# Attention with a gated MLP on one core: a planned order of the engines' queues, and part of the softmax exponentials computed on VectorE

## The chip, the cores and the metric

One core of a Trainium2 chip runs the whole program. The metric is the device time of one execution in microseconds (us). TensorE (PE) multiplies, ScalarE (ACT) computes functions such as the exponential, VectorE (DVE) does element-wise work, GpSimd (POOL) a little of it, SyncE (SP) issues most transfers.

## The reference

```python
def _A_ref(x, wqkv, wo):                      # S = 2048, D = 640, H = 32, Dh = 20
    qkv = (x @ wqkv).reshape(B, S, 3, H, Dh)  # -> q, k, v
    p = softmax(einsum("bhqd,bhkd->bhqk", q, k) * Dh ** -0.5)
    return einsum("bhqk,bhkd->bhqd", p, v).reshape(B, S, D) @ wo
def _B_ref(x, w1, b1, w2):                    # F = 1536
    h = einsum("bsd,df->bsf", x, w1) + b1
    return einsum("bsf,fd->bsd", h * tanh(softplus(h)), w2)     # Mish
g = sigmoid((x * gate_w).sum(-1, keepdims=True))
return g * _A_ref(x, wqkv, wo) + (1 - g) * _B_ref(x, w1, b1, w2)
```

All tensors are bf16. The softmax needs 32 x 2048 x 2048 exponentials.

## The kernel before

Four heads are taken together (`p`, 8 packs), each in 32 partitions, and 512 query columns (`qc`, 4 chunks): 32 groups. In a group, 16 key tiles of 128 (`j`) times 4 heads (`t`) make 64 units; a unit is a 128x512 block of scores. Units are taken alternately three and two at a time. One such iteration is a score step on PE (L568; up to four heads sit in different rows of the array and run together) into one of two PSUM tiles, and one exponential on ACT (L578). The 4 heads of a key tile are then multiplied with V in one V step (L609; four column strips together), summed in the PSUM tile `acc`. V carries a column of ones, so the sum of the exponentials comes out too. After 16 key tiles the group is transposed on DVE, divided and transposed back (`normalise`, L584).

Everything else is "chains" on PE: Q and K (L243) and V (L264) projections, the first MLP product (L327), the second (L356) and the output projection (L393). Each chain fills one of two PSUM tiles (`pp`), which DVE empties. A chain has a start and a due time in iterations; `pump` (L541) issues, after each iteration, as many chain pieces as the shares ask for, at most 700 ns of them. The Mish of each 128x512 block of `h` is spread over the following iterations (L289): an exponential on ACT, then on DVE a polynomial, four reciprocals (L304) and products.

PE, ACT and DVE each work their queues in order, so an instruction that waits holds all behind it.

Of the kernel before, what the change touches and what calls it, by code (L numbers as in the profile page):

```python
# [9 lines left out]
P = 128  # L10
# [3 lines left out]
BF16 = mybir.dt.bfloat16  # L14
PSUM = bass.MemoryType.PSUM


class Chain:

    def __init__(self, start, due, pieces, finish, ready=None, hard=True):
        self.start, self.due, self.pieces, self.finish = start, due, deque(pieces), finish
        self.ready = ready or (lambda: True)
        self.hard = hard
        self.cost = sum(c for c, _ in pieces)

    def share(self, i):
        if i >= self.due:
            return self.cost  # L30
        if i <= self.start:
            return 0.0
        return self.cost * (i - self.start) / (self.due - self.start)
# [3 lines left out]
def kernel(  # L37
# [26 lines left out]
    WIDTHS = (3, 2)  # L64
    N_CAP = 1.0e30
# [19 lines left out]
    actp = ctx.enter_context(tc.tile_pool(name="actp", bufs=16))
    outp = ctx.enter_context(tc.tile_pool(name="outp", bufs=2))
# [23 lines left out]
    w1t = {}  # L110

    def load_strip(kind, p, eng):
        t = wsp.tile([P, KT, 4 * DH], BF16, tag=f"ws{kind}", name="ws")
        c0 = kind * D + p * 4 * DH
        eng.dma_start(out=t[:, :, :], in_=wrows[:, :, c0 : c0 + 4 * DH])  # L115
        strips[(kind, p)] = t

    def load_w1(k):
        if k < 4 * NQC:
            i = k % 4  # L120
            w1t[k] = w1p.tile([P, KT, 3 * P], BF16, tag="w1t", name="w1t")
# [12 lines left out]
    for c in range(1, NQC):  # L134
        nc.sync.dma_start(
            out=xs[c][:, :, :],
            in_=x2d[c * QC : (c + 1) * QC, :].rearrange("(u p) d -> p u d", p=P),
        )
# [16 lines left out]
    for t in (wqp[1], wkp[1], T2[0], T2[1]):  # L155
        nc.gpsimd.memset(t, 0.0)
# [10 lines left out]
    first = {}  # L167
    for G, (p, qc) in enumerate(groups):
        first.setdefault(p, G)
    units = [  # L170
        (G, p, qc, j, t)
        for G, (p, qc) in enumerate(groups)
        for j in range(NS)
        for t in range(4)
    ]
    iters = []
    pos = 0
    while pos < len(units):
        n = min(WIDTHS[len(iters) % len(WIDTHS)], len(units) - pos)
        iters.append((pos, n))  # L180
        pos += n
    NI = len(iters)
    it_of = [0] * len(units)
    for i, (a, n) in enumerate(iters):
        for k in range(a, a + n):
            it_of[k] = i

    def it_at(G, j=0):
        k = G * 64 + 4 * j
        return it_of[k] if k < len(units) else NI  # L190

    kT = {}
    qT = {}
    OT = {}
    Bt = {}
    act = {}
    later = []
    seq = [0]
    in_mish = [0]
    b_done = [0] * NQC  # L200
    normalised = set()
    x_ready = [NU] + [0] * (NQC - 1)

    def at(i, fn):
        seq[0] += 1
        later.append((i, seq[0], fn))

    now = [0]


    def mm_pieces(n, fn, each):
        return [(each, (lambda k=k: fn(k))) for k in range(n)]

    def transpose_tile(c, u, ps, eng):
        s = NU * c + u
        for kt in range(KT):
            nc.tensor.transpose(  # L217
                ps[:, kt * P : (kt + 1) * P], xs[c][:, u, kt * P : (kt + 1) * P], ident
            )
        dst = xT[:, :, s * P : (s + 1) * P]  # L220
        src = ps[:, 0 : KT * P].rearrange("p (k q) -> p k q", q=P)
        if eng is nc.scalar:
            nc.scalar.copy(out=dst, in_=src)
        else:
            eng.tensor_copy(out=dst, in_=src)  # L225

    def transpose_chain(c, u, start, due):
        def piece():
            ps = pp.tile([P, KT * P], BF16, tag="pp", name="ps")
            transpose_tile(c, u, ps, nc.vector)  # L230
            x_ready[c] += 1

        return Chain(start, due, [(400, piece)], lambda: None)

    def kq_chain(wpad, chunk, get_dst, start, due, before=None, copy=None):
        box = {}

        def piece(kt):
            if kt == 0:
                if before is not None:  # L240
                    before()
                box["ps"] = pp.tile([P, QC], F32, tag="pp", name="ps")
# [3 lines left out]
                rhs=xT[:, kt, chunk * QC : (chunk + 1) * QC],  # L246
# [4 lines left out]
        def finish():  # L251
            (copy or nc.vector.tensor_copy)(out=get_dst(), in_=box["ps"][:, :])  # L252

        return Chain(start, due, mm_pieces(KT, piece, 215), finish, lambda: x_ready[chunk] == NU)

    def v_chain(sts, w, c0, n, start, due, gate=False):
        box = {}
        width = n + (1 if gate else 0)

        def piece(k):  # L260
            i, kt = divmod(k, KT)
            if k == 0:
                box["ps"] = pp.tile([P, len(sts), width], F32, tag="pp", name="ps")
# [9 lines left out]
        def finish():  # L273
            h0 = 0 if gate else c0 // DH
            nh = n // DH
            for i, st in enumerate(sts):
                nc.vector.tensor_copy(
                    out=VA[:, st, h0 : h0 + nh, 0:DH],
                    in_=box["ps"][:, i, 0:n].rearrange("p (h d) -> p h d", d=DH),
                )  # L280
            if gate:
                nc.vector.tensor_copy(
                    out=z_t[:, sts[0] : sts[0] + len(sts)], in_=box["ps"][:, :, n]
                )

        return Chain(start, due, mm_pieces(KT * len(sts), piece, max(40, width / 2.3)), finish,
                     lambda: all(x_ready[st // NU] == NU for st in sts))

    def mish_steps(ft, c, h):  # L289
        e = mp.tile([P, QC], F32, tag="e", name="e")  # L290
        r = mp.tile([P, QC], F32, tag="r", name="r")
        nc.scalar.activation(e[:, :], h[:, :], ACT.Exp)  # L292

        def first_ops():
            nc.vector.scalar_tensor_tensor(  # L295
                out=e, in0=e, scalar=2.0, in1=e, op0=ALU.add, op1=ALU.mult
            )
            nc.vector.tensor_scalar(
                out=r, in0=e, scalar1=N_CAP, scalar2=2.0, op0=ALU.min, op1=ALU.add
            )  # L300

        def rec(k):
            a, b = k * P, (k + 1) * P
            nc.vector.reciprocal(out=r[:, a:b], in_=r[:, a:b])  # L304

        def last_ops():
            nc.vector.scalar_tensor_tensor(
                out=r, in0=e, scalar=N_CAP, in1=r, op0=ALU.min, op1=ALU.mult
            )
            t = actp.tile([P, QC], BF16, tag="act", name="act")  # L310
            nc.vector.tensor_tensor(out=t, in0=h, in1=r, op=ALU.mult)
            act[(ft, c)] = t
            in_mish[0] -= 1

        at(now[0] + 1, first_ops)
        for k in range(4):
            at(now[0] + 2 + k, (lambda k=k: rec(k)))
        at(now[0] + 6, last_ops)

    def h_chain(ft, c, start, due):  # L320
        box = {}

        def piece(kt):
            if kt == 0:
                in_mish[0] += 1
                box["ps"] = pp.tile([P, QC], F32, tag="pp", name="ps")
            nc.tensor.matmul(  # L327
                box["ps"][:, :],
                lhsT=w1t[4 * c + ft // 3][:, kt, (ft % 3) * P : (ft % 3 + 1) * P],
# [3 lines left out]
            )  # L333

        def finish():
# [5 lines left out]
            if ft % 3 == 2:  # L341
                load_w1(4 * c + ft // 3 + 2)
# [397 lines left out]
```

## Time and profile before

| | |
|---|---|
| time, median of 3 runs | 1138.24 us (1133.45 to 1138.47) |
| span of the profiled execution | 1130.1 us; its own time is not given apart from the span |
| mean granted TensorE clock | 0.667 of 2.4 GHz |
| busy: PE, ACT, DVE, POOL | 1036.3, 992.6, 490.7, 16.2 us |
| PE matmuls / ACT / DVE instructions | 5545 recorded / 873 / 767 |

An engine's busy time is the union of its instructions; PE's matmuls are pipelined, so steps are better read by the distance of their starts. The granted clock is 1.00 (2.4 GHz) or 0.50 (1.2 GHz) at any moment; a value between is a mean over a stretch.

### The profile page before, as it was taken

To read this page: it belongs to the slowest core of one execution; us is meant where nothing else is said; L and a number is where in the kernel's file an instruction comes from. 1 tells how busy PE (TensorE), PEld (TensorE's weight loads), DVE (VectorE), ACT (ScalarE), POOL (GpSimd) and SP (SyncE) were. 2 spreads that over 40 slices of the span, in tenths; PEclk is the share of its full clock that TensorE was granted. 3 is DMA by queue.
4 is the path that set the end of the run, shared out by engine and by line. 5 is a ranking of instruction groups with operands and counts; after the bars stand their busy time and mean duration, and the time that the engine had idled before them with its cause. 6 is when DMAs were issued, how large, how long until landed. Compare 5 with 4: busy or idle time off the path is not lost.

```text
span 1130.1 us, 13823 instructions
## 1 busy us (share of the span) xinstructions
PE 1036.3 (92%) x5545; PEld 267.9 (24%) x5616; DVE 490.7 (43%) x767; ACT 992.6 (88%) x873; POOL 16.2 (1%) x26
## 2 busy tenths in 40 slices
PE   6898789999899999989999999899999989998996
PEld 3322221123212112321111123111112321212232
DVE  3336675612665655225665532465556211011123
ACT  4988998889988888998888899988988998889896
POOL 2000000000000000000100000000000000000000
PEclk8866965579656555985555589555556975557688
DMA  8000001000010001000020000000000000000000
GB/s 252 2 1 18 18 1 26 18 1 1 1 25 18 18 1 25 1 1 18 1 54 18 11 15 1 1 18 17 1 1 1 1 1 12 7 12 6 13 19 30
DMA packets 31272, 19.35 MB, mean 17 GB/s; under 512 B 14056, under 2 KB 31208, under 8 KB 31208
## 3 DMA queue, kind: packets, MB, share of 16 engines
q1 hardware_dynamic: 28664, 17.60, 5.7%
q10 hardware_dynamic: 2544, 0.86, 0.3%
q8 instruction: 44, 0.72, 0.3%
q14 instruction: 20, 0.16, 0.1%
HBM read 15.84 MB, written 2.62 MB: 16 GB/s over the span
## 4 chain that ended last, share of the span: by engine, by line
PE 64%; ACT 22%; issue 11%; DVE 2%; DMA 1%; SPq 0%; ACTq 0%; DVEq 0%
PE Sp L568 24%; ACT E L578 21%; PE acc L609 15%; PE ps L243 8%; PE ps L327 7%; PE ps L393 4%; PE ps L264 3%; PE ps L356 2%; ACT e L292 1%; DMA b1bf<-in_B_b_dram 1%; DMA ws<-in_A_wqkv_dram 0%; DVE r L304 0%; SPq L115 0%; PE ps L217 0%; DVE ot L699 0%
## 5 line engine op out<-in xcount | busy, mean ns | idle before, releaser
L578 ACT ACTIVATE E<-Sp 128x1536 bf16<-128x1536 f32 (+1 forms) x819 | 967.9, 1245 | 113.3 <-PE Sp L568 67.0
L568 PE MATMUL Sp<-qT,kT 32*128 32x512 bf16 x2048 | 430.1, 519 | 71.1 <-ACT E L578 55.2
L609 PE MATMUL acc<-E,VA 128*21 128x512 bf16 x2048 | 270.9, 519 | 1.0 <-ACT E L578 1.0
L568 PEld LDWEIGHTS <-kT 32*128 32x128 bf16 x2048 | 97.0, 96 | 366.5 <-issue 360.3
L304 DVE RECIPROCAL r<-r 128x128 f32<-128x128 f32 x192 | 168.3, 919 | 1.3
L327 PE MATMUL ps<-xT,w1t 128*128 128x512 bf16 x208 | 116.1, 571 | 0.5 <-issue 0.5
L609 PEld LDWEIGHTS <-VA 128*21 128x21 bf16 x2048 | 51.6, 91 | 184.8 <-issue 184.8
L356 PE MATMUL ps<-w_sb,act 128*128 128x320 bf16 x384 | 81.2, 318 | 0.0
L337 DVE TENSOR_SCALAR h<-ps,b1f 128x512 f32<-128x512 f32 x48 | 35.4, 738 | 105.5 <-PE ps L327 105.5
L243 PE MATMUL ps<-xT,wqp 128*128 128x512 bf16 x134 | 70.2, 549 | 1.8 <-issue 1.8
L393 PE MATMUL ps<-wo_sb,OT 128*128 128x320 bf16 x248 | 70.5, 379 | 0.0
L367 DVE TENSOR_SCALAR Bt<-ps,g_t 128x320 bf16<-128x320 f32 x32 | 17.6, 550 | 118.4 <-PE ps L356 118.2
L243 PE MATMUL ps<-xT,wkp 128*128 128x512 bf16 x137 | 64.8, 504 | 1.9 <-issue 1.0
L295 DVE SCALAR_TENSOR_TENSOR e<-e 128x512 f32<-128x512 f32 x48 | 33.0, 687 | 58.7 <-ACT e L292 58.6
L409 DVE SCALAR_TENSOR_TENSOR ot<-ps,g_t,Bt 128x320 bf16<-128x320 f32 x24 | 13.2, 551 | 103.5 <-PE ps L393 103.5
L586 DVE STREAM_TRANSPOSE T<-acc 128x512 f32<-128x512 f32 x32 | 22.9, 717 | 75.8 <-PE acc L609 75.8
L252 DVE CAST qT<-ps 128x512 bf16<-128x512 f32 x31 | 21.3, 687 | 73.1 <-PE ps L243 70.2
L264 PE MATMUL ps<-wv,xT 128*128 128x81 bf16 (+2 forms) x240 | 48.9, 314 | 4.2 <-DVE xT L225 4.2
L327 PEld LDWEIGHTS <-w1t 128*128 128x128 bf16 x240 | 23.0, 103 | 84.4 <-issue 84.4
L252 DVE CAST kT<-ps 128x512 bf16<-128x512 f32 x31 | 21.1, 682 | 38.6 <-PE ps L243 38.5
L356 PEld LDWEIGHTS <-act 128*128 128x128 bf16 x384 | 28.4, 100 | 38.4 <-issue 32.3
L292 ACT ACTIVATE e<-h 128x512 f32<-128x512 f32 x48 | 30.1, 628 | 4.5 <-DVE h L337 4.5
(55 smaller groups left out, 274.1 us busy)
## 6 DMA issues: line engine op xcount, KB each, us to landing
w1t<-in_B_w_dram SPq DMA_DIRECT2D x16, 480.0 KB, 3.8
out_dram<-ot SPq DMA_DIRECT2D x14, 160.0 KB, 1.8
xs<-in_A_x_dram SPq DMA_DIRECT2D x3, 640.0 KB, 7.4
w_sb<-in_B_w_dram SPq DMA_DIRECT2D x1, 1920.0 KB, 9.8
ws<-in_A_wqkv_dram SPq DMA_DIRECT2D x15, 100.0 KB, 4.0
wv<-in_A_wqkv_dram SPq DMA_DIRECT2D x1, 800.0 KB, 9.8
wo_sb<-in_A_wo_dram SPq DMA_DIRECT2D x4, 200.0 KB
xs<-in_A_x_dram ACTq DMA_DIRECT2D x2, 160.0 KB, 3.2
```

The source lines that it names most:

```text
L243: nc.tensor.matmul(box["ps"][:, :], lhsT=wpad[:, kt, :, :].rearrange("p h d -> p (h d)"), rhs=xT[:, kt, chunk * QC : (chunk + 1) * QC], st ...
L252: (copy or nc.vector.tensor_copy)(out=get_dst(), in_=box["ps"][:, :])
L264: nc.tensor.matmul(box["ps"][:, i, :], lhsT=xT[:, kt, sts[i] * P : (sts[i] + 1) * P], rhs=w[:, kt, c0 : c0 + width], start=(kt == 0), stop ...
L292: nc.scalar.activation(e[:, :], h[:, :], ACT.Exp)
L304: nc.vector.reciprocal(out=r[:, a:b], in_=r[:, a:b])
L327: nc.tensor.matmul(box["ps"][:, :], lhsT=w1t[4 * c + ft // 3][:, kt, (ft % 3) * P : (ft % 3 + 1) * P], rhs=xT[:, kt, c * QC : (c + 1) * QC ...
L337: nc.vector.tensor_scalar(out=h, in0=box["ps"][:, :], scalar1=b1f[:, ft : ft + 1], scalar2=None, op0=ALU.add)
L356: nc.tensor.matmul(box["ps"][:, :], lhsT=act[(ft, c)][:, u * P : (u + 1) * P], rhs=w2_sb[:, ft, half * HALF : (half + 1) * HALF], start=(f ...
L393: nc.tensor.matmul(box["ps"][:, :], lhsT=OT[p][:, s * P : (s + 1) * P], rhs=wo_sb[0][:, p, cols], start=(k == 0), stop=(k == len(ps_list) ...
L568: nc.tensor.matmul(ps[:, k * QC : (k + 1) * QC], lhsT=kT[p][32 * t : 32 * t + 32, j * P : (j + 1) * P], rhs=qT[G][32 * t : 32 * t + 32, :] ...
L578: nc.scalar.activation(E[:, 0 : n * QC], S_of.pop(i)[:, 0 : n * QC], ACT.Exp, scale=inv_sqrt_dh)
L609: nc.tensor.matmul(acc[32 * t : 32 * t + DH + 1, :], lhsT=VA[:, j, 4 * p + t, :], rhs=E_of.pop(a + t), start=(j == 0), stop=(j == NS - 1), ...
```

## The change

All queue orders are now written by a planner (L1132 on), which steps through time with estimated costs for each engine and issues what is ready there. The two PSUM tiles of the score steps, the two of the chains and the slots in SBUF are tracked by when they come free.

In addition, per group up to 5 key tiles ("sets") are taken from the end of the group's list for DVE, 94 of 512 in all. Their score rows go one at a time into a chain's PSUM tile. DVE scales and offsets a row and writes it as a 16-bit integer, whose bits read as bf16 are about the exponential (`power`). Three more copies with 32, 64 and 96 added to the integer (`shift`) differ from it in phase; each of the four is multiplied with V, the three shifted ones with a V scaled by a constant (`VD`), and `acc` sums them, so the errors of the four average out. Such a set costs four V steps in place of one.

The Mish is no longer done by blocks of 128x512. All 12 blocks of a chunk of 512 rows are collected in bf16; then ACT runs exp, ln(1 + e) and tanh over them, three instructions of 2048 columns each, and DVE multiplies by `h`. Attention rows go out to DRAM after normalisation and are loaded again in dense tiles of 128 rows, so the output projection has 5 matmuls instead of 8. The MLP result goes through DRAM too.

```diff
+    SHIFT = (0, 32, 64, 96)
+    RATIO = (1.0, 0.83984375, 0.70703125, 0.59375)
+    ND = 5
+            nc.vector.tensor_scalar(
+                out=VD[p][:, :, i, :],
+                in0=VA[:, NS - ND : NS, 4 * p : 4 * p + 4, :].rearrange("p j h d -> p j (h d)"),
+                scalar1=RATIO[i + 1], scalar2=None, op0=ALU.mult,
+            )
...
+    def d_unit(t, bank, used):
+        for d in d_open:
+            for r in sorted(d["rows"] - used):
...
+                ps = psum.tile([P, QC], F32, tag=bank.tag, name="ps")
+                score(ps[:, :], d["G"], d["j"], r)
+                def power(t, d=d, r=r, ps=ps):
+                    nc.vector.tensor_scalar(
+                        out=d["T"][:, r * QC : (r + 1) * QC].bitcast(I16), in0=ps[:, :],
+                        scalar1=inv_sqrt_dh * LOG2E * 128.0, scalar2=127.0 * 128.0 + BETA,
+                        op0=ALU.mult, op1=ALU.add,
+                    )
...
+    def d_shifts(d, t):
...
+            nc.vector.tensor_scalar(
+                out=tile_[:, :].bitcast(I16), in0=d["T"][:, :].bitcast(I16),
+                scalar1=float(SHIFT[i]), scalar2=None, op0=ALU.add,
+            )
...
-        nc.scalar.activation(e[:, :], h[:, :], ACT.Exp)
...
-            nc.vector.reciprocal(out=r[:, a:b], in_=r[:, a:b])
...
+        def func(k, fn, bias):
+            v = e_t[c][:, HB * k : HB * k + HB, :].rearrange("p f q -> p (f q)")
+            nc.scalar.activation(v, v, fn, bias=bias)
...
+    def emit_pv(it, t):
...
+                i, tile_, slot = it[2]
+                rhs = tile_[:, t_ * QC : (t_ + 1) * QC]
+                if i:
+                    lhsT = VD[p][:, j - (NS - ND), i - 1, t_ * (DH + 1) : (t_ + 1) * (DH + 1)]
...
+    def step_pe(t):
+        units = s_ready(t)
...
+            emit_s(units, t + cost - MM)
+            for b in fb:
+                if d_unit(t + cost - MM, b, used):
```

PE, before, in the middle of the first MLP product (`w1t`): score steps (`Sp`), V steps (`acc`) and chain matmuls (`ps`) alternate.

```order
L609 MATMUL acc<-E,VA 21x512
L243 LDWEIGHTS wqp_113
L243 MATMUL ps<-xT,wqp_113 128x512
L327 LDWEIGHTS w1t
L327 MATMUL ps<-xT,w1t 128x512 [waits DVE_49]
L568 LDWEIGHTS kT
L568 MATMUL Sp<-qT,kT 128x512 [waits Activation_49]
L568 LDWEIGHTS kT
L568 MATMUL Sp<-qT,kT 128x512
L327 LDWEIGHTS w1t
L327 MATMUL ps<-xT,w1t 128x512
```

PE, now, near the middle of the program: `T` is a tile of integers from DVE, `VD` the scaled V.

```order
L916 LDWEIGHTS VD
L916 MATMUL acc<-T,VD 21x512
L839 LDWEIGHTS kT
L839 MATMUL Sp<-qT,kT 128x512 [waits Activation_49]
L839 LDWEIGHTS kT
L839 MATMUL Sp<-qT,kT 128x512
L839 LDWEIGHTS kT
L839 MATMUL ps<-qT,kT 128x512 [waits DVE_49]
L916 LDWEIGHTS VA
L916 MATMUL acc<-E,VA 21x512
```

A score row for DVE (`ps`) joins the score step and waits for DVE to have emptied its tile; V steps of T stand beside those of E.

ACT, before, around one block of the Mish (`e`):

```order
L578 ACTIVATE E<-Sp 128x1536 [waits PE_49,Activation_49]
L578 ACTIVATE E<-Sp 128x1024 [waits PE_49,Activation_49]
L292 ACTIVATE e<-h 128x512 [waits DVE_49]
L578 ACTIVATE E<-Sp 128x1536 [waits PE_49,Activation_49]
L578 ACTIVATE E<-Sp 128x1024 [waits PE_49,Activation_49]
```

ACT, now, around the Mish of the first chunk:

```order
L878 ACTIVATE E<-Sp 128x1024 [waits PE_49,Activation_49]
L504 ACTIVATE e<-e 128x2048 [waits DMAHW2_49,DMAHW1_49,DVE_49]
L504 ACTIVATE e<-e 128x2048 [waits DVE_49] x2
L504 ACT_TABLE_LOAD
L504 ACTIVATE e<-e 128x2048 [waits Activation_49] x3
L504 ACT_TABLE_LOAD
L504 ACTIVATE e<-e 128x2048 [waits Activation_49] x3
L878 ACTIVATE E<-Sp 128x1536 [waits PE_49]
```

Single exponentials of the Mish between those of the softmax became one block of nine activations and two table loads.

## Rows read from the trace of the kernel before

**Rows 1.** The page, parts 1 and 4: busy us and share; the chain.

```profile
PE 1036.3 (92%) x5545; PEld 267.9 (24%) x5616; DVE 490.7 (43%) x767; ACT 992.6 (88%) x873; POOL 16.2 (1%) x26
...
PE 64%; ACT 22%; issue 11%; DVE 2%; DMA 1%; SPq 0%; ACTq 0%; DVEq 0%
```

**Rows 2.** Windows: stretch, its length, busy us (x instructions) by engine, PEclk, DMA.

```profile
503.00:660.00 157.00, 149.68 (x652) 29.69 (x663) 94.86 (x138) 136.25 (x122) 5.28 (x3) 0.50 0.09 21
660.00:711.00 51.00, 45.45 (x335) 16.48 (x335) 8.60 (x16) 51.00 (x45) 0.98 (x2) 1.00 0.00 1
```

**Rows 3.** Windows of the exponentials' line L578 alone.

```profile
12.90:28.25 15.35, 8.68 (x8) 0.78 0.83 232
28.25:122.00 93.75, 80.44 (x70) 0.76 0.02 6
...
503.00:660.00 157.00, 131.38 (x111) 0.50 0.09 21
660.00:711.00 51.00, 51.00 (x45) 1.00 0.00 1
```

**Rows 4.** Timeline of PE, 228 to 241 us: start, us, line, [idle].

```profile
228.11 0.98 PE L356 MATMUL ps<-w_sb,act 128*128 128x320 bf16 x3
229.02 0.61 PE L568 MATMUL Sp<-qT,kT 32*128 32x512 bf16 x2
229.56 0.61 PE L609 MATMUL acc<-E,VA 128*21 128x512 bf16 x4
...
240.37 0.60 PE L243 MATMUL ps<-xT,wqp 128*128 128x512 bf16 x2
240.91 0.39 PE L568 MATMUL Sp<-qT,kT 32*128 32x512 bf16 x3
```

**Rows 5.** Timeline of PE at 259 us.

```profile
259.08 0.39 PE L568 MATMUL Sp<-qT,kT 32*128 32x512 bf16 x3 [0.19 <-ACT E L578]
259.41 0.40 PE L609 MATMUL acc<-E,VA 128*21 128x512 bf16 x4
259.73 0.58 PE L356 MATMUL ps<-w_sb,act 128*128 128x320 bf16 x3
260.25 0.39 PE L568 MATMUL Sp<-qT,kT 32*128 32x512 bf16 x2
```

**Rows 6.** Timeline of PE at 291 us.

```profile
290.40 0.31 PE L264 MATMUL ps<-wv,xT 128*128 128x320 bf16 x1
291.61 0.61 PE L568 MATMUL Sp<-qT,kT 32*128 32x512 bf16 x3 [0.90 <-ACT E L578]
```

**Rows 7.** Timeline of PE at 655 us.

```profile
654.71 1.03 PE L243 MATMUL ps<-xT,wkp 128*128 128x512 bf16 x2
655.68 0.61 PE L568 MATMUL Sp<-qT,kT 32*128 32x512 bf16 x3
```

**Rows 8.** Lines by form, ACT: busy us, mean ns of one, idle before.

```profile
L578 ACT ACTIVATE E<-Sp 128x1536 bf16<-128x1536 f32 x410 | 597.6, 1458 | 90.2 <-PE Sp L568 46.8 <-PE acc L609 39.9 <-PE ps L327 0.2
...
L578 ACT ACTIVATE E<-Sp 128x1024 bf16<-128x1024 f32 x409 | 422.0, 1032 | 23.0 <-PE Sp L568 20.2 <-PE acc L609 0.7
...
L150 ACT ACT_TABLE_LOAD x1 | 1.3, 1283 | 4.3 <-DMA xs<-in_A_x_dram 4.3
```

**Rows 9.** Lines by form, DVE.

```profile
L304 DVE RECIPROCAL r<-r 128x128 f32<-128x128 f32 x192 | 168.3, 919 | 1.3
...
L252 DVE CAST qT<-ps 128x512 bf16<-128x512 f32 x31 | 21.3, 687 | 73.1 <-PE ps L243 70.2 <-PE Sp L568 1.5 <-PE acc L609 1.5
...
L298 DVE TENSOR_SCALAR r<-e 128x512 f32<-128x512 f32 x48 | 20.5, 427 | 1.6
...
L277 DVE CAST VA<-ps 128x80 bf16<-128x80 f32 x16 | 2.7, 236 | 4.2 <-PE ps L264 4.2
...
L159 DVE COPY wkp<-ws 128x400 bf16<-128x400 bf16 x1 | 0.3, 255 | 0.0
```

**Rows 10.** Timeline of ACT, the last exponentials.

```profile
1106.60 12.82 ACT L578 ACTIVATE E<-Sp 128x1536 bf16<-128x1536 f32 x11 [0.40 <-PE acc L609]
```

More of the change, by code (lines that the diff above doesn't have):

```diff
@@ L166 @@
     groups += [(p, qc) for qc in range(NQC) for p in (NQ - 2, NQ - 1)]
-    first = {}
+    NG = len(groups)
+    first, last = {}, {}
     for G, (p, qc) in enumerate(groups):
         first.setdefault(p, G)
[L170 to L181, printed above, removed]
@@ L208 @@
-    now = [0]
-    def mm_pieces(n, fn, each):
[L212 to L238, printed above, removed]
+        last[p] = G
+    kT, qT = {}, {}
+    k_ready = {}
+    q_ready = {}
+    v_ready = {}
+    x_ready = {}
@@ new lines, with dve @@
+    e_ready = {}
+    banks = [Slot("pa"), Slot("pb")]
+    tile_free = {"X": 0.0, "Y": 0.0}
+    EX = {"X": [Slot(f"EX{i}") for i in range(4)], "Y": [Slot(f"EY{i}") for i in range(4)]}
+    ex_next = {"X": 0, "Y": 0}
+    dve_q = []
+    act_q = deque()
+    seq = [0]
+    free = {"PE": 0.0, "ACT": 0.0, "DVE": 0.0}
+    mode = [None]
+    prog = [0.0]
+    s_left = [64] * NG
+    idle = {"PE": 0.0, "ACT": 0.0, "DVE": 0.0}
+    def dve(t, ready, cost, fn, prio=1, done=None, can=None):
+        seq[0] += 1
+        dve_q.append((prio, ready, seq[0], cost, fn, done, can))
@@ L280, in finish @@
                 )
+            ops = [(60.0 + n, (lambda t, i=i: copy(i, t))) for i in range(len(sts))]
             if gate:
[L282 to L291, printed above, removed]
-        nc.scalar.activation(e[:, :], h[:, :], ACT.Exp)
[L294 to L303, printed above, removed]
-            nc.vector.reciprocal(out=r[:, a:b], in_=r[:, a:b])
[L306 to L318, printed above, removed]
@@ L601 @@
[L601 to L621 removed]
+    AHEAD = 0.0
@@ new lines @@
+    steps = {"PE": step_pe, "ACT": step_act, "DVE": step_dve}
+    t = 0.0
+    stuck = 0
+    vd_next = 0
+    while pv_G[0] < NG or chains or chain[0] or dve_q or act_q:
+        any_ = False
+        if vd_next < NQ and prog[0] > first[vd_next] - 1.0 and (
+            vd_next < 2 or pv_G[0] > last[vd_next - 2]
+        ) and all(v_ready.get((vd_next, st), INF) <= t for st in range(NS - ND, NS)):
+            make_vd(vd_next, t)
+            vd_next += 1
+        for ev in list(events):
+            if ev[0](t):
+                events.remove(ev)
+                ev[1](t)
+        for eng in ("DVE", "ACT", "PE"):
+            if free[eng] <= t:
+                cost = steps[eng](t)
+                if cost is None:
+                    idle[eng] += 20.0
+                else:
+                    free[eng] = t + cost
+                    any_ = True
+        stuck = 0 if any_ else stuck + 1
+        assert stuck < 2000, "the order came to a standstill"
+        t += 20.0
@@ L709 @@
         )
+    if DEBUG:
+        print("model end us", t / 1e3, {k: v / 1e3 for k, v in idle.items()}, "sets", sum(n_d), n_d)
 _INS = ['A_x', 'A_wqkv', 'A_wo', 'B_x', 'B_w1', 'B_b1', 'B_w2', 'gate_w']
```

1018 lines of the change are left out of this document (702 added, 316 removed).

## The prediction

> **What bounds the kernel now.** I read the page's busy shares and its chain first, then the clock by stretches, then single steps of PE at both clock levels.
>
> The page gives PE 92%, ACT 88%, DVE 43% of the span, and a chain that runs 64% through PE and 22% through ACT [rows 1]. Two engines near 90% look like one balanced kernel; the stretches show two regimes instead. In 660 to 711 us the granted clock is 1.00 (2.4 GHz): ACT is busy 51.00 of 51.00 us and PE 45.45. In 503 to 660 us it is 0.50 (1.2 GHz): PE is busy 149.68 of 157 us and ACT only 136.25 [rows 2]. So ACT bounds at the full clock and PE at the half clock. In score exponentials (the activation at L578): 45 in 51.00 us is 1.133 us each at the full clock, 111 in 157 us is 1.41 us each at the half one [rows 3]. The mean clock over the span is 0.667, so about two thirds of the span run in the slow regime.
>
> What PE did before the clock moved is in three places. It rose at about 240 us: at 228 us steps of 512 columns still take 0.54 us, the second product of the MLP runs in threes between the score and V steps without a gap, and at 240.37 two 512-column steps take 0.54 together [rows 4]. In the full-clock stretch at 259 us the same pattern goes on [rows 5]. It fell at about 291 us, when a single matmul stood before the next score step and PE then waited 0.90 us for ACT [rows 6]. So this kernel falls when, at full clock, PE has too little to do beside ACT's pace, and then PE becomes the bound.
>
> **Step prices of PE.** A "step" is a set of up to four row- or column-tiled matmuls that start together, or one full-size matmul. Half clock: 512 columns and then another kind of step, 0.54 us (229.02 to 229.56); three of 320 columns, 0.91 (228.11 to 229.02) [rows 4]; two of 512 of one kind, 0.97, so 0.43 where the kind stays [rows 7]. Full clock: 0.32 with a change of kind, three of 320 in 0.52 [rows 5]; two of 512 of one kind 0.54, so 0.22 where it stays [rows 4].
>
> **The change, part by part.**
>
> ACT. The new queue holds 334 exponentials of 1536 and 335 of 1024 columns instead of 410 and 409 [rows 8]; 376 of 2048 units (94 sets) leave. 669 x 1.133 = 758 us at ACT's own pace. The Mish now costs ACT three functions on 2048 columns, 36 in all: from 1024 to 1536 columns the duration grows 426 ns, so 2048 take about 1458 + 426 = 1.88 us, less an overlap of 0.11 (two exponentials last 1.458 + 1.032 = 2.49 and take 2 x 1.133 = 2.27), 1.77 x 36 = 64 us. Eight table loads at 1.283 are 10 us [rows 8]. ACT's sum: 832 us. The Trainium skill (ScalarE: Activation LUTs, "What ACT_TABLE_LOAD costs") adds about 1.38 us of drain to each switch of set; no row here shows that, and by it the sum would be 11 us longer.
>
> DVE. 192 reciprocals of 919 ns, 168 us busy of DVE's 491, go [rows 1, 9]. New are 376 conversions of 128x512 from PSUM, like the cast at L252, 0.687 us: 258 us. And 282 shifts of 128x2048 of 16-bit integers inside SBUF, which no row shows. Casts of 80 and 512 elements from PSUM take 236 and 687 ns: 1.04 ns an element on top of some 152 ns. By that rate a shift takes 2.3 us. The f32 operation in SBUF at L298 takes 427 ns for 512, so 0.54 an element on the same 152, and gives 1.25 us. The 16-bit copy in SBUF at L159 takes 255 ns for 400, 0.26 an element, and gives 0.68 us [rows 9]. I take 0.69, by the row nearest in type and place, and keep 2.3 as the far end. The sum: 491 - 168 + 258 + 282 x 0.69 = 776 us at most (the other small Mish steps shrink too). That lies beside ACT's 832.
>
> The Trainium skill (VectorE: DVE Perf Modes, "The perf-mode tier table") has one-source operations on 16-bit data in SBUF at four results a cycle, 693 ns for 2048; the copy row agrees with that in size. It would not change the sum.
>
> PE. Counted in the order: 770 score steps and 794 V steps (before 819 and 512), as a set done on DVE needs four V steps instead of one; the output projection drops from 256 to 168 matmuls. Of the 512-column steps, 1495 are followed by another kind and 629 by the same; of 320 columns there are 631; the small ones come to about 19 us at full clock and 34 at half. Full clock: 1495 x 0.32 + 629 x 0.22 + 631 x 0.173 + 19 = 745 us. Half clock: 1495 x 0.54 + 629 x 0.43 + 631 x 0.303 + 34 = 1303 us. So at full clock PE (745) hides behind ACT (832); at half clock it is the bound again and by more than before.
>
> Which clock? The extra V steps are what speaks for the full one. While ACT is paced at 1.133 us an exponential, PE now has 745/669 = 1.11 us of full-clock steps beside each; where the clock fell at 291 us, it had gaps of 0.90 us [rows 6]. The order also has longer runs of one kind (V steps of E and of T one behind the other), as before the rise at 240 us [rows 4].
>
> One place of the change speaks against it. Nine Mish activations and two table loads stand together in ACT's queue, four times: 16 + 2.6 = 18.5 us without one exponential, in which PE has only leftover steps and waits for ACT. Behind such a wait the clock fell at 291 us [rows 6], so I let it fall at each of the four. In the old kernel the second MLP product brought it back within some 12 us (228 to 240) [rows 4]; that product follows each Mish here too. I take 15 us low each time: PE does 745/1303 = 0.57 of the work, 6.4 us are lost, in all 26 us. The Trainium skill (TensorE: Matmul & The Clock Gate, "What's actually happening") says that "the default state is throttled, and activity releases the throttle". The fall at 291 us and the rise at 240 us agree; by it four falls are to be expected, and the sum stays.
>
> SP gets 124 small stores of attention rows and 32 of the MLP result with its reloads, on a queue of some 227 transfers instead of 57 (counted in the order). Each store waits for DVE, and behind it on SP stand the weight strips, which are asked for one pack of heads ahead. I cost it at nothing, hidden by that lead; a strip that came late would stop one chain, and if that chain holds Q or K, PE's whole queue.
>
> The sum. Engines that are both nearly full do not overlap perfectly: where PE bounds, it still loses 5% (149.68 of 157 busy) [rows 2]; at 89% load beside ACT nothing is lost. PE's 745 less some 30 us inside the four Mish stretches, over 832 - 74 = 758, is a load of 94%. I take the 5%: 832 / 0.95 = 876. Start: first exponential at 12.9 us, then 8 in 15.35 us (6.3 lost); 70 in the following 93.75 us lose 14 more against 1.133 each [rows 3]; both kept, 33. Falls behind the Mish 26. Tail: the last exponential of before ends at 1106.60 + 12.82 = 1119.4 and the span at 1130.1, 11 us [rows 10]; kept. 876 + 33 + 26 + 11 = 946 us of span. The runs' median of 1138.2 lies 8 above the profiled span, so 954 us.
>
> **The rivals.**
>
> 1. PE held up by DVE. PE's queue is in order, and each score row for DVE needs one of two PSUM banks that DVE must have emptied (the wait for DVE at `ps` in the order). Before, 214 chains used these banks (counted in the code); now 376 rows more. Behind a waiting row stand V steps and the next score step, for which ACT waits. For it: DVE at 776 of some 900 us is busy when such a row comes up about as often as not, and a shift or transpose in front takes 0.7 us. Against: DVE has 10% to spare. If each row held PE a quarter of a microsecond: 376 x 0.25 = 94, so 1048 us.
>
> 2. The clock stays low (the slower side). Place: the stretches behind each Mish and those of the first MLP product. At half clock throughout, 1303 / 0.95 + 44 (start and tail) + 8 = 1424 us. Linear between 954 and 1424, it passes the 1138 of before when 39% of the work runs at 1.2 GHz. For it: before spent two thirds so, and 157 us at a time [rows 2]. Against: in those stretches single steps of changing kind stood in the queue, 0.54 us each, and every stretch with runs came back.
>
> 3. The shifts run at a lower rate. For it: no row shows 16-bit integers. Against: the copy row [rows 9]. At 1.25 us DVE has 581 + 353 = 934 us and bounds: 934 / 0.95 + 44 + 8 = 1035. At 2.3 it has 1230 and the time is 1347. It passes 1138 at 1.6 us a shift.
>
> 4. The engines overlap without the 5%, and the clock holds: 832 + 33 + 11 + 8 = 884. For it: ACT busy 51.00 of 51.00 beside a PE at 89% [rows 2]; against: PE is at 94% here.
>
> **How the numbers follow.** The forecast, 895 to 1010 us, has 0.68; rival 1, to 1080, 0.14; rival 2, 0.09, of which 0.07 above 1138; rival 3, 0.05, of which 0.02 above; rival 4, 0.04. Faster by over 0.5%, about what a measurement of this kernel can tell from no change: 0.68 + 0.14 + 0.02 + 0.03 + 0.04 = 0.91. Of the 0.09 left, 0.01 lies within 0.5% and 0.08 is slower. The range that holds 8 in 10 is 895 to 1080: it leaves out rival 4 and what of rivals 2 and 3 is past 1080, some 0.15.
>
> **What would show it.** Right: a mean granted clock of 0.85 or more, low only behind the four groups of Mish activations; ACT busy over 90% outside the start; shifts of about 0.7 us; PE's busy V line near 794 steps of 0.32. Wrong: clock 0.50 in a stretch with first MLP products (rival 2); PE's waits for DVE in the hundreds of us (rival 1); shifts over 1.2 us (rival 3). If ACT is idle although PE runs at full clock and DVE is not late, the 5% was too small.

## The result, and the profile after

The changed kernel takes 892.65 us (median; 891.91 to 893.39) against 1138.36 us (1133.45 to 1138.5) before, a ratio of 0.785 [0.7825, 0.7872]. The direction and the regime were as forecast, but 892.65 lies below the range of 895 to 1080 us. Of the rivals it lies nearest to 4 (884 us): hardly any of the 5% was lost, but the clock did not hold throughout as that rival had it, and that it comes within 9 us of 884 is in part luck, since other terms were off both ways. One execution of 3513 us, of the six of the repeat of experiment 10, is left out of that ratio.

The page of the changed kernel, its span, busy times, clock by slice and chain:

```profile
span 891.5 us, 16303 instructions
...
PE 816.6 (92%) x6656; PEld 257.2 (29%) x6656; DVE 642.6 (72%) x1101; ACT 839.0 (94%) x719; POOL 13.6 (2%) x26
...
PEclk9999995899999976999999959999999779999988
...
ACT 47%; PE 32%; issue 15%; DVE 3%; DMA 2%; SPq 0%; ACTq 0%; DVEq 0%
```

PE has the same share as before (92%), yet the chain has gone from 64% PE to 47% ACT [rows 1]: the busy share of PE did not show which engine bounds, the clock did. The mean granted clock is 0.935 (0.667 before), and it falls for long at four places. The stretches around the first of these and three between them (stretch, length, then busy us by engine PE, PEld, DVE, ACT, POOL, with instructions; granted clock; DMA):

```profile
132.00:151.40 19.40, 12.51 (x69) 2.63 (x66) 16.82 (x28) 19.34 (x13) 0.00 (x0) 0.64 0.09 16
151.40:175.20 23.80, 22.29 (x173) 5.78 (x172) 18.52 (x31) 20.98 (x19) 0.00 (x0) 0.79 0.00 1
175.20:320.00 144.80, 142.18 (x1171) 44.10 (x1170) 100.20 (x169) 144.80 (x129) 1.98 (x4) 1.00 0.08 22
363.00:507.00 144.00, 140.80 (x1179) 44.67 (x1175) 109.53 (x181) 140.84 (x126) 1.47 (x2) 1.00 0.12 32
550.60:690.00 139.40, 137.41 (x1157) 42.00 (x1145) 103.31 (x173) 139.40 (x125) 0.99 (x2) 1.00 0.08 21
```

132 to 151.4 us is a Mish on ACT: ACT is full and PE has 12.51 us of work. In the 23.8 us behind it ACT is busy 20.98, so 2.8 us are lost. In the long stretches at 1.00 ACT is busy 144.80 of 144.80 us, and 139.40 of 139.40, while PE stands at 98% of them. Before, with PE at 89%, ACT was full for 51 us [rows 2]; now it is beside a PE that shows 98%. That is not a load of 98%: experiment 12 puts 1256 matmuls into 140 us where 1157 stand in 139.40 here.

The Mish itself, on ACT's timeline (start, us, line, [idle before and what ended it]):

```profile
132.05 5.69 ACT L504 ACTIVATE e<-e 128x2048 bf16<-128x2048 bf16 x3
137.76 1.28 ACT L504 ACT_TABLE_LOAD   x1
139.06 5.51 ACT L504 ACTIVATE e<-e 128x2048 bf16<-128x2048 bf16 x3
...
151.30 4.60 ACT L878 ACTIVATE E<-Sp 128x1536 bf16<-128x1536 f32 x4
157.21 2.52 ACT L878 ACTIVATE E<-Sp 128x1536 bf16<-128x1536 f32 x2 [1.31 <-PE Sp L839]
161.19 4.62 ACT L878 ACTIVATE E<-Sp 128x1536 bf16<-128x1536 f32 x4 [1.46 <-PE Sp L839]
```

Three activations last 5.5 us (1.84 each), a load 1.28, and the next activation starts 0.02 us behind the load. ACT then waits twice for PE, which is at the low clock (0.50, 1.2 GHz) to 161.6 us, and not again before the next Mish.

The lines by form that answer to [rows 8] and [rows 9] (busy us, mean ns, idle before):

```profile
L878 ACT ACTIVATE E<-Sp 128x1536 bf16<-128x1536 f32 x334 | 514.5, 1540 | 26.5 <-PE Sp L839 15.6 <-PE acc L916 6.3 <-PE ps L839 4.5
L878 ACT ACTIVATE E<-Sp 128x1024 bf16<-128x1024 f32 x335 | 374.9, 1119 | 4.4 <-PE acc L916 2.0 <-PE Sp L839 1.8 <-PE ps L839 0.5
...
L296 DVE TENSOR_SCALAR T<-ps 128x512 int16<-128x512 f32 x376 | 256.2, 686 | 162.3 <-PE ps L839 150.6 <-PE Sp L839 9.1
L321 DVE TENSOR_SCALAR T<-T 128x2048 int16<-128x2048 int16 x282 | 182.6, 685 | 2.3 <-PE acc L916 0.5
```

ACT waits 31 us in all for its 669 exponentials; 113 us before. The two DVE operations, conversion and shift, last 686 and 685 ns.

The waits that the rivals spoke of (us in total, times, longest):

```profile
PE Sp L839 <- ACT E L878: 22.5, 42, 3.8
ACT E L878 <- PE Sp L839: 17.4, 17, 2.7
PE acc L916 <- DVE T L321: 12.0, 17, 1.7
PE ps L839 <- DVE T L296: 9.6, 12, 2.1
PE acc L916 <- DVE T L296: 4.2, 5, 2.7
...
ACT E L878 <- PE acc L916: 8.3, 3, 3.2
...
PE ps L631 <- DMA od<-o_dram: 3.3, 2, 2.3
```

PE waits for DVE some 26 us in these three lines, not the 94 of rival 1; DVE in turn waits 150.6 us for PE's rows. The last line is PE waiting for attention rows that are loaded again from DRAM (`od`).

### The profile page after: what moved, and what is told of

It is laid out like the page before. It is cut to its first block, busy times and chain, and to the rows that moved or that the text cites. A ratio compares the mean times of both kernels' runs of the same rounds, so it can differ in the third digit from the quotient of the medians.

```text
span 891.5 us, 16303 instructions
## 1 busy us (share of the span) xinstructions
PE 816.6 (92%) x6656; PEld 257.2 (29%) x6656; DVE 642.6 (72%) x1101; ACT 839.0 (94%) x719; POOL 13.6 (2%) x26
## 4 chain that ended last, share of the span: by engine, by line
ACT 47%; PE 32%; issue 15%; DVE 3%; DMA 2%; SPq 0%; ACTq 0%; DVEq 0%
ACT E L878 39%; PE acc L916 10%; PE Sp L839 9%; ACT e L504 7%; PE ps L378 3%; PE ps L458 3%; PE ps L553 2%; PE ps L839 2%; PE ps L631 2%; PE ps L402 2%; ACT L504 1%; DMA od<-o_dram 1%; DMA b1bf<-in_B_b_dram 1%; DVE T L321 1%; DVE T L296 0%
## 5 line engine op out<-in xcount | busy, mean ns | idle before, releaser
L878 ACT ACTIVATE E<-Sp 128x1536 bf16<-128x1536 f32 (+1 forms) x669 | 760.2, 1329 | 30.9 <-PE Sp L839 17.4
L296 DVE TENSOR_SCALAR T<-ps 128x512 int16<-128x512 f32 x376 | 256.2, 686 | 162.3 <-PE ps L839 150.6
L839 PE MATMUL Sp<-qT,kT 32*128 32x512 bf16 x1672 | 268.9, 392 | 27.3 <-ACT E L878 22.5
L321 DVE TENSOR_SCALAR T<-T 128x2048 int16<-128x2048 int16 x282 | 182.6, 685 | 2.3 <-PE acc L916 0.5
L916 PE MATMUL acc<-E,VA 128*21 128x512 bf16 x1672 | 165.6, 395 | 2.1 <-DVE VA L418 1.9
L839 PE MATMUL ps<-qT,kT 32*128 32x512 bf16 x376 | 148.3, 412 | 9.6 <-DVE T L296 9.6
L916 PE MATMUL acc<-T,VD 128*21 128x512 bf16 x1128 | 108.3, 412 | 12.0 <-DVE T L321 12.0
L553 PE MATMUL ps<-w_sb,e 128*128 128x320 bf16 x384 | 79.3, 305 | 0.5 <-DVE T L296 0.5
L504 ACT ACTIVATE e<-e 128x2048 bf16<-128x2048 bf16 x36 | 66.8, 1960 | 0.1
L916 PE MATMUL acc<-T,VA 128*21 128x512 bf16 x376 | 44.1, 415 | 4.2 <-DVE T L296 4.2
```

What stands on the lines that cost most here:

```text
L296: nc.vector.tensor_scalar(out=d["T"][:, r * QC : (r + 1) * QC].bitcast(I16), in0=ps[:, :], scalar1=inv_sqrt_dh * LOG2E * 128.0, scalar2=12 ...
L321: nc.vector.tensor_scalar(out=tile_[:, :].bitcast(I16), in0=d["T"][:, :].bitcast(I16), scalar1=float(SHIFT[i]), scalar2=None, op0=ALU.add,)
L504: nc.scalar.activation(v, v, fn, bias=bias)
L553: nc.tensor.matmul(box["ps"][:, :], lhsT=e_t[c][:, ft, u * P : (u + 1) * P], rhs=w2_sb[:, ft, half * HALF : (half + 1) * HALF], start=(ft ...
L839: nc.tensor.matmul(ps_cols, lhsT=kT[p][32 * t_ : 32 * t_ + 32, j * P : (j + 1) * P], rhs=qT[G][32 * t_ : 32 * t_ + 32, :], tile_position=( ...
L878: nc.scalar.activation(E[:, 0 : n * QC], ps[:, 0 : n * QC], ACT.Exp, scale=inv_sqrt_dh)
```

## Experiments

Each was timed beside the kernel before on the same chip; the ratios are to that.

**1. The planned order without the sets.**

```diff
-    ND = 5
+    ND = 0
-    vd_next = 0
+    vd_next = NQ
```

> The planned order, the collected Mish and the dense output projection stay, but no set goes to VectorE: 819 exponentials on ACT as before, 512 V steps. Theory A (the extra V steps and the shorter ACT work together keep TensorE at 2.4 GHz): PE has only about 684 us of full-clock steps (counted in the order, priced as in the prediction) beside 819 x 1.122 + 77 = 996 us of ACT, so the clock falls in long stretches, mean granted clock under 0.80, time over 1080 us. Theory B (the planned order alone overlaps the engines, the clock follows): clock 0.90 or more and about 996 + 25 (start) + 12 (tail) + 10 = 1043 us.

Measured: 1149.54 us, 1.0106 [1.0069, 1.0142]. The page:

```profile
PE 899.4 (78%) x5528; PEld 265.5 (23%) x5528; DVE 233.7 (20%) x419; ACT 1022.1 (89%) x869; POOL 12.5 (1%) x26
...
PEclk9999856888597857988779668876888568697775
```

As theory A has it. Everything in the change but the sets makes the kernel no faster. The clock frays all over (mean 0.782), and PE waits for ACT 227.7 us.

**2. The sets without their extra V steps.**

```diff
-        pv_total[G] += 3
-                done=lambda t, i=i: pv_items[G].append((t, j, (i,) + d["T%d" % i])),
+                done=lambda t, i=i: release(d["T%d" % i][1], t),
```

> As the changed kernel, sets and shifts on VectorE included, but the three V steps of each set's shifted copies are left out, so its output lacks their part of the sum. ACT 663 x 1.122 + 77 = 821 us, PE about 682 us of full-clock steps in place of 745. Theory A (the extra V steps are what holds the clock): mean clock clearly under the 0.935 of the changed kernel, 0.85 or less, and a time over 900 us although there is less to do. Theory B (less beside ACT is enough once the order is dense): clock 0.92 or more, 870 to 885 us.

Measured: 882.21 us, 0.7728 [0.7682, 0.7774], mean clock 0.912, ACT busy 832.2 us, PE 768.9 (87%). The reason that I gave for the full clock, that the extra V steps hold it, is not needed: with ACT's work cut by the sets, the clock nearly holds without them, and ACT still sets the time.

**3. Useless work in the kernel before.** Each V step is followed by one with zero weights.

```diff
+            for t in range(4):
+                nc.tensor.matmul(
+                    acc[32 * t : 32 * t + DH + 1, :], lhsT=Z[:, :], rhs=E_of.pop(a + t),
+                    start=False, stop=(j == NS - 1), tile_position=(0, 32 * t),
+                )
```

> The kernel before, with each V step followed by a second one whose weights are zeros (2048 more matmuls, nothing else changed; the sums stay). Theory A (what bounds the kernel before is TensorE's clock, and that follows how much PE streams): mean clock over 0.85 in place of 0.667, ACT-paced at 1.13 us an exponential for most of the span, 990 to 1060 us, faster than 1138 with a third more matmuls. Theory C (PE is the bound and more work on it costs its price): clock as before, 512 x 0.43 x two thirds + 512 x 0.22 x one third = 184 us longer, about 1320 us.

Measured: 1041.84 us, 0.9138 [0.9097, 0.9178]. The page:

```profile
PE 913.2 (88%) x7664; PEld 281.7 (27%) x7664; DVE 490.0 (47%) x768; ACT 970.6 (93%) x873; POOL 17.0 (2%) x26
...
PEclk9999988999999999999999999989999999999998
```

512 more V steps, and PE is busy 123 us less than before (913.2 against 1036.3 [rows 1]), at a clock of 0.969. What cost the kernel before 96 us was that PE had too little to do at full clock, not too much.

**4. The same with one and a half zero steps a V step,** to see whether more helps.

```diff
+            nz = 1 + j % 2
+            for z in range(nz):
```

> The kernel before with one zero V step behind each V step and two behind every second: PE's full-clock steps 911 us beside ACT's 954, 95% load, in the old order. If engines near 95% load lose 5% as the prediction took it: ACT idle grows from zero_v's 70 to about 100 us, 1065 us or more. If a full PE costs ACT nothing: 1035 to 1048 us.

Measured: 1056.63 us, 0.9265 [0.9234, 0.9295], clock 0.983. Three of its stretches (columns as above):

```profile
200.00:300.00 100.00, 95.42 (x874) 29.79 (x877) 38.57 (x60) 94.36 (x83) 0.99 (x2) 1.00 0.03 8
430.00:530.00 100.00, 94.50 (x850) 28.48 (x847) 48.10 (x74) 95.01 (x86) 5.38 (x3) 0.98 0.02 6
590.00:690.00 100.00, 93.34 (x864) 29.11 (x852) 38.70 (x59) 96.13 (x87) 1.40 (x2) 1.00 0.04 8
```

Between the two expectations. In the old order, with PE at 93 to 95% of a stretch at or near full clock, ACT is busy 94 to 96%. But these 4 to 6% are not a price of load as the 5% of my sum was, as what ended ACT's waits in the whole run shows (us in total, times, longest):

```profile
ACT E L580 <- PE acc L622: 32.4, 91, 2.1
ACT E L580 <- PE Sp L570: 16.5, 27, 4.4
```

L622 is a zero step: it reads a tile of E, which ACT can write again only behind it. It ends 10.3 of the 14.5 us that ACT stands in the three stretches. So most of that loss is ACT waiting for a free tile of E, which the experiment's own steps hold longer. With fewer zero steps (experiment 3) the first of these stretches loses 2.6%:

```profile
200.00:300.00 100.00, 93.25 (x796) 28.39 (x797) 42.21 (x65) 97.38 (x88) 0.98 (x2) 1.00 0.06 13
```

In the planned order ACT loses nothing or 2% (144.80 of 144.80, 140.84 of 144.00).

**5. The planned order without sets, with zero steps behind each V step.**

```diff
-    ND = 5
+    ND = 0
-                cost = (SWITCH if mode[0] != "V" else 0.0) + MM
+                cost = (SWITCH if mode[0] != "V" else 0.0) + 2 * MM
```

The four zero matmuls are those of experiment 3, in `emit_pv`.

> The changed kernel without sets on VectorE, each V step followed by one whose weights are zeros: ACT's work as in no_sets (819 exponentials), PE's full-clock steps 809 us in place of 684. Theory A (no_sets is slow because its clock flips): clock over 0.95 and 996 + 25 + 12 + 10 = 1043 us, some 105 us faster than no_sets with 2048 more matmuls; what then remains to the changed kernel's 893, about 150 us, is ACT's shorter work (150 exponentials by 1.122 = 168, less 18). Theory F (no_sets is slow because the planner's order without sets is bad): 1149 us or more.

Measured: 1059.66 us, 0.9304 [0.9264, 0.9344], clock 0.914, ACT busy 1012.2 us: far from theory F, short of A's clock and 17 us above its time. Against experiment 1 the zero steps give 0.080 of the time of before (91 us). From here to the changed kernel it is 0.146 (166 us); 869 - 719 = 150 ACT instructions fewer, at (1012.2 - 839.0) / 150 = 1.15 us each, are 173 us. So the 246 us of the change are, in ratios, as these three kernels divide them: the order +0.011, the clock -0.080, the exponentials that ACT no longer does -0.146. The clock of 0.914 here was not a whole one, so some of the last part may still be the clock's.

**6. Two sets a group in place of five,** 62 in all.

```diff
-    ND = 5
+    ND = 2
```

> At most two sets a group in place of five, 62 in all (counted in the order): 720 exponentials on ACT. If the clock holds: 720 x 1.122 + 77 + 47 = 932 us, mean clock 0.93 or more (ACT's price alone, 0.449 us a unit, 128 units more than the changed kernel: +57 less waits). If the clock frays at this load (PE 735 us of full-clock steps beside 808 of exponentials, 91%): clock 0.85 to 0.90 and 950 to 990 us.

Measured: 960.22 us, 0.8404 [0.8365, 0.8443]; clock 0.897, ACT busy 900.4. With fewer sets ACT has more to do, PE less, and the clock frays again.

**7. The same 62 sets, and zero V steps where the planner has nothing for PE.**

```diff
+        if prog[0] > 0.5 and G < NG and 0 < pv_done[G] < pv_total[G] and acc_free[0] <= t:
+            for t_ in range(4):
+                nc.tensor.matmul(
+                    acc[32 * t_ : 32 * t_ + DH + 1, :], lhsT=Z[:, :], rhs=xT[:, 0, 0:QC],
+                    start=False, stop=False, tile_position=(0, 32 * t_),
+                )
+            mode[0] = "V"
+            return MM
```

> At most two sets a group (62 in all), with zero V steps wherever the planner has nothing for PE (584 of them). Without them the same 62 sets took 960 us at a mean clock of 0.90, ACT busy 900 us. Theory A (what 960 has over ACT's 900 is the clock's fraying): clock 0.97 or more and about 937 us (900 + 13 ahead of the first exponential + 12 behind the last + 12 lost at the start). Rival (the order around late work, not the clock): 955 or more.

Measured: 939.29 us, 0.8248 [0.822, 0.8275]. The page:

```profile
PE 903.9 (96%) x8608; PEld 296.9 (32%) x8608; DVE 508.9 (54%) x878; ACT 902.0 (96%) x770; POOL 12.6 (1%) x26
...
PEclk8999999999999999999999999999999999999998
```

ACT's work is the same (902.0), the clock 0.99, and 0.016 of the time of before is gone (18 us; 21 between the medians, which are of two chips). The forecast of 937 was worked out from ACT's sum alone: the clock was what 960 had over it.

**8. A score exponential between the Mish functions,** so that ACT's queue holds no block without one; the planner then takes 89 sets.

```diff
-        if act_q and act_q[0][0] <= t:
+        if act_q and act_q[0][0] <= t and (turn[0] or ln_left[0] % 3 or not S_q):
+            turn[0] = False
...
-            return emit_exp(t)
+            cost = emit_exp(t)
+            if cost is not None:
+                turn[0] = True
+            return cost
```

> As the changed kernel, but ACT takes a score exponential between two Mish activations (the three logarithms stay together, so two table loads per chunk as before). Theory D (the falls of the clock behind the four Mish blocks cost the 9.4 us that ACT stands idle in those stretches): no such fall, clock over 0.97, 880 to 886 us. Rival E (the block only moves PE's slack about; PE at 98% beside ACT has none to give): clock higher, time within 0.5% of 892.6 or above it.

Measured: 903.16 us, 0.79 [0.7851, 0.7948]; the clock (mean 0.92) still falls at each Mish and is low there for 41, 27, 17 and 27 us. Interleaving does not hold it, so neither expectation on the clock came; ACT's busy time is 848.8 us, 10 more for the five sets lost. That ACT empties a score tile there only with every other activation is a likely reason, not tested.

**9. Sets later in a group:** it may still give one when four key tiles are left; 99 sets.

```diff
-    DMIN = 7
+    DMIN = 4
```

> The changed kernel with sets taken until four key tiles are left in a group's list instead of seven: 99 sets (counted in the order), 20 units fewer on ACT, 15 more V steps. If ACT is still the bound: 20 x 0.449 = 9 us less, 884 us. If PE (98% busy between the Mish blocks) has become it: 893 to 900 us.

Measured: 915.81 us, 0.8037 [0.8008, 0.8066], although ACT has 832.1 us of work. In the waits `ACT E` for `acc` has 29.1 us, up to 7.00 at once. PE's timeline ahead of one such wait, which ends at 281.60:

```profile
276.68 0.84 PE L402 MATMUL ps<-wv,xT 128*128 128x320 bf16 x5
277.45 0.40 PE L916 MATMUL acc<-T,VA 128*21 128x512 bf16 x4
278.10 0.40 PE L916 MATMUL acc<-T,VD 128*21 128x512 bf16 x4 [0.25 <-DVE T L321]
278.50 0.37 PE L839 MATMUL ps<-qT,kT 32*128 32x512 bf16 x1
279.10 0.40 PE L916 MATMUL acc<-T,VD 128*21 128x512 bf16 x4 [0.23 <-DVE T L321]
279.70 0.40 PE L916 MATMUL acc<-T,VD 128*21 128x512 bf16 x4 [0.21 <-DVE T L321]
280.30 0.37 PE L839 MATMUL ps<-qT,kT 32*128 32x512 bf16 x1 [0.20 <-DVE T L296]
280.92 1.89 PE L916 MATMUL acc<-E,VA 128*21 128x512 bf16 x16 [0.25 <-DVE T L937]
```

A set taken late ends its group: the three shifts come from DVE one by one, `acc` closes only behind them, and the next group's four V steps wait for its transpose (L937). All that time the E tiles are full and ACT stands. Here a wait of DVE does reach the end, by the way that rival 1 did not name.

**10. Zero V steps while a Mish runs:** the edit of experiment 7 under another condition; `DMIN` 6 keeps 94 sets.

```diff
-    DMIN = 7
+    DMIN = 6
+        if t <= mish_end[0] and G < NG and 0 < pv_done[G] < pv_total[G] and acc_free[0] <= t:
+            mish_end[0] = t + cost + 1500.0
```

> The changed kernel, with V steps whose weights are zero put where the planner has nothing for PE while a Mish runs on ACT (207 such steps, 94 sets as in the changed kernel; DMIN is 6 in place of 7 so that the number of sets stays). Theory A (the clock falls because PE runs out of work while the Mish holds ACT): the four stretches of 24 us at half clock go, and with them the 9 us that ACT stands idle behind them: about 883 us. Theory D (the fall has another cause, or it costs nothing that the end feels): 890 us or more, and the low stretches stay.

Measured: 888.94 us, 0.7807 [0.7782, 0.7833], clock 0.99: between A's 883 and D's 890, with A's clock. The first and the last of the stretches that hold a Mish, and the one before the last:

```profile
132.00:175.00 43.00, 41.73 (x465) 14.08 (x461) 36.32 (x61) 42.94 (x34) 0.00 (x0) 1.00 0.07 16
...
550.00:690.00 140.00, 136.39 (x1144) 41.88 (x1143) 107.97 (x181) 136.49 (x121) 0.98 (x2) 1.00 0.07 19
690.00:738.00 48.00, 44.79 (x506) 15.19 (x502) 38.24 (x63) 47.62 (x38) 0.00 (x0) 1.00 0.09 27
```

No fall is left at a Mish, and ACT is busy 42.94 of 43.00 us where the changed kernel has 40.3 of 43.2. But 3.5 us are lost in 550 to 690, where nothing was lost. It is a single wait for `acc` (3.51 us, up to 666.11), behind the three shifted V steps that end a group: the kind of experiment 9.

**11. The same at 89 sets** (`DMIN` left at 7), as many as in experiment 8.

> The same zero steps during the Mish with DMIN left at 7; the planner then takes 89 sets, as in the kernel with exponentials between the Mish functions, so ACT has eight more exponentials, 9 us. Theory A: no fall at the Mish, about 892 us. Theory D: 900 us or more.

Measured: 890.86 us, 0.7821 [0.7791, 0.7852], clock 0.984, ACT busy 847.2 us. With the same sets and the same work on ACT it is 0.008 of the time of before (9 us) below experiment 8; the two intervals just touch, and the order of ACT's queue differs too.

**12. Zero V steps everywhere that PE's model is idle** (94 sets, `DMIN` 5).

> Zero V steps wherever the planner has nothing for PE after the start (432 of them, 94 sets, DMIN 5). Theory A: the clock holds from some 30 us on, ACT is idle only at the start and the end: 878 to 885 us. Rival: a full PE queue delays the score steps, as in the kernel before with one and a half zero steps a V step: over 892 us.

Measured: 910.46 us, 0.7992 [0.7961, 0.8023], clock 0.99. Late in the kernel (same columns):

```profile
550.00:690.00 140.00, 139.23 (x1256) 41.22 (x1253) 101.99 (x171) 138.80 (x122) 0.98 (x2) 1.00 0.08 20
...
738.00:870.00 132.00, 128.79 (x1239) 42.33 (x1236) 93.28 (x157) 118.68 (x104) 0.00 (x0) 0.99 0.17 52
```

The time is the rival's, but its reason is not shown. 738 to 870 us has ACT at 118.68 of 132 (127.17 in the changed kernel), and most of that is lost in two of ACT's waits:

```profile
771.60 24.33 ACT L880 ACTIVATE E<-Sp 128x1536 bf16<-128x1536 f32 x21 [2.72 <-PE acc L918]
802.64 5.54 ACT L880 ACTIVATE E<-Sp 128x1024 bf16<-128x1024 f32 x5 [6.71 <-PE acc L918]
```

Both are for `acc`, and ahead of the longer one PE's timeline shows what experiment 9 shows: the V steps of one more set, the transpose, then 16 matmuls of V steps of E at once. In all ACT waits 24.6 us for `acc` (29.1 in experiment 9, 8.3 in the changed kernel), but 11.9 for score steps (17.4 there). So `DMIN` 5 is a likelier cause than the fill, which in experiment 7, with `DMIN` 7 and PE at 96%, brings no wait for `acc`; fill everywhere with 94 sets and `DMIN` 7, or `DMIN` 5 alone, was not run.

**13 to 16. Four kernels beside each other on one chip:** the changed kernel; `DMIN = 6` alone (95 sets); experiment 10 again; and its zero steps with `DMIN` 7 and `DALONE = 8000` (93 sets; the planner then sends single score rows for DVE earlier).

> The changed kernel itself, as the measure for the three kernels beside it on this chip: 893 us, both theories.

> DMIN 6 in place of 7 (95 sets), no zero steps: what the kernel with zero steps during the Mish differs from but for them. Theory C (a lower DMIN puts sets late in a group, and ACT waits for the group behind them, as with DMIN 4 at 23 us): 895 to 903 us. Theory D (DMIN 6 costs nothing): 889 to 893 us.

> The zero V steps during the Mish again, DMIN 6, 94 sets, beside the changed kernel on one chip. Theory A (holding the clock through the Mish gives back what ACT lost behind it, less what DMIN 6 costs): 4 us below the changed kernel, and 8 or more below DMIN 6 without zero steps. Theory D: equal to both.

> The zero V steps during the Mish with DMIN 7; DALONE 8000 in place of 2000 keeps the sets at 93. ACT has three exponentials more than in the changed kernel, 3.4 us. Theory A with C: no late sets and no fall, 885 to 888 us. Theory D: 893 us or more.

Measured, in this order: 891.76 us (889.0 to 892.8), ratio 0.7833 [0.7793, 0.7873]; 893.01 (891.62 to 897.44), 0.7853 [0.7816, 0.7889]; 890.23, 0.7823 [0.7785, 0.7861]; 900.13 (897.41 to 902.07), 0.7909 [0.7868, 0.7949]. `DMIN` 6 costs nothing that can be told, and its ACT is busy 139.40 of 139.40 us at 550 to 690; but ACT waits 12.8 us for `acc` in all, at other places (4.36 us up to 301.92), so the wait of experiment 10 is of a kind that `DMIN` 6 has without zero steps too. Holding the clock through the Mish is 1.5 us below the changed kernel, inside both intervals: theory D's "equal to both", no gain is shown on one chip, although its trace again has 43.14 of 43.20 us busy at the first Mish. The last one is slower, on theory D's side (893 or more), by more than its three exponentials (3.4 us); its waits point to a cause:

```profile
PE Sp L841 <- ACT E L880: 24.2, 54, 1.4
ACT E L880 <- PE ps L841: 20.3, 13, 3.9
ACT E L880 <- PE Sp L841: 14.5, 13, 3.7
```

ACT waits 20.3 us for rows for DVE (`ps`) that stand in PE's queue ahead of a score step, 4.9 in the changed kernel. That the earlier rows alone do it was not tested. No version was shown to beat the changed kernel.

## Why the prediction missed, step by step

The span of 891.5 us against the terms of the sum:

| term | predicted | measured |
|---|---|---|
| ACT's own work | 832 | 835.6 |
| imperfect overlap of PE and ACT (the 5%) | 44 | 9.0 (3.2 in 363 to 507 us; 5.8 after 738 us, see the reloads below) |
| start (before the first exponential, and up to 132 us) | 33 | 25 (12.9 + 12.1) |
| behind the four Mish blocks | 26 | 9.4 |
| tail | 11 | 12.4 |

**The failed step is "I take the 5%".** It alone is 35 of the 55 us between 946 and 891.5. By itself it would have left 919 us, inside the range; the falls (17 us too dear), the start (8) and the 8 us between span and time, which measured 1.9 (893.39 against 891.5), did the rest. The 5% came from a stretch at half clock where PE bounds [rows 2], in the old order, and was put on a kernel where ACT bounds, in a new order. The stretch of 144.80 us shows that it does not hold there, and experiment 4 does not confirm it for the old order either: its 4 to 6% are in the main waits for free tiles of E. The 3.2 us are such a wait too, one of 3.11 us up to 439.85, where a group that ends with a set closes. ACT's waits of this kind were far more in the kernel before:

```profile
ACT E L578 <- PE acc L609: 40.5, 73, 1.0
```

One difference that the text ahead of the prediction does not name bears on it: E has eight tiles in the new kernel (`EX`, four of each width) and had four (`ep`). That these make the order better, and not its mix of pieces, the set slots or the score rows joined to score steps, was not tested. The only row with ACT as the bound, 51.00 of 51.00 [rows 2], pointed to rival 4, and I gave it 0.04.

**The reloads** are a term that the prediction put at nothing: it thought of the weight strips on SP's queue, not of the attention rows that the output projection needs back. PE waits for them twice in the middle of its queue, 2.30 us up to 840.51 and 1.02 up to 865.45. Each time the clock falls (840.8 to 844.3, 864.7 to 871.6), and all of ACT's waits after 738 us, 5.8 us, lie between 839 and 874. The chain has these loads too (`od`, 1%).

**The falls behind the Mish** came, four, as said, and only there, but for a short dip at the start and those at the end. They lasted longer than I took (23.9 us against 15) and cost less (2.35 us each against 6.4): about 14 us of each lie inside the Mish, when ACT needs nothing of PE. I charged all of the low time to the end. Experiment 11 against 8 prices the falls of experiment 8, with its interleaving, at some 9 us, the repeat of 10 against the changed kernel on one chip at 1.5, which can't be told from none; between these it stays open.

**Why the clock holds** was half wrong. That PE needs enough to do beside ACT's pace is shown (experiments 3, 5 and 7, each with useless work alone). That the extra V steps give it is not needed (experiment 2): less work on ACT brings PE nearer to it too.

**Right:** the ACT sum (exponentials 760.2 us busy, 758 predicted; the Mish 66.8 and 64); the shifts, 685 ns for 0.69, so rival 3 is out. The Trainium skill (VectorE: DVE Perf Modes, "The perf-mode tier table") gives four results a cycle for 2048 bf16 elements in SBUF, 693 ns, and the trace's 685 for 16-bit integers agrees. DVE's 776 us "at most" became 642.6, in the main since the other Mish steps shrank too. No wait for a weight strip shows after the start, so SP's stores did not delay those.

The 11 us that the sum would be longer by the Trainium skill (ScalarE: Activation LUTs, "What ACT_TABLE_LOAD costs") are not there: the next activation starts 1.30 us behind the start of a load of 1.28.

**Rival 2** (the clock stays low) did not come with five sets a group; it shows in experiments 1 and 6. Rival 1 was too dear at a quarter of a microsecond a row; DVE had 28% to spare, not 10%.

## What to carry to other kernels

Take the loss between two nearly full engines from a stretch where the same engine bounds as in the new kernel; if none loses anything, nought is the likelier value and the loss is the range. Look at what ends the waiting engine's waits before you call a loss the price of load: here it was free tiles and reloads. PE's clock fell here when PE ran short of work (0.667 in mean before, 0.969 with useless work in experiment 3), so "less work" and "faster" are two things: price a change at both clocks, and try filler work to see which one you are in. A stretch at the low clock costs only that part in which the bounding engine waits for it.

## What had not been expected of the hardware

- Matmuls that add nothing make the kernel before 8.6% faster (experiment 3), and fill of PE's gaps takes 18 us from experiment 6.
- A Mish block leaves the clock low for 23.9 us each of the four times (137.7 to 161.6 us for the first), and for some 21 to 27 us in the repeat (experiment 13).
- Away from such a block the clock can fray too: it went up and down in spells of some 3 to 45 us through all of experiment 1.
- PE at 98% busy was not full: fill put 1256 matmuls into 550 to 690 us with ACT still at 138.80 of 140.00 (experiment 12). What ACT lost later in that run it lost in waits for `acc`.
